# A product kernel whose moving tiles begin a few words behind an aligned place

## The chip, the cores and the metric

The kernel runs on one core of a Trainium2 chip. The metric is the device time of one execution in microseconds (us). On this core TensorE multiplies, VectorE and ScalarE do elementwise work and take results out of PSUM, and the SP queue issues the DMAs. SBUF is the memory on the chip that the engines read; a place in it is given here as a partition's byte address, and a word is 4 bytes.

## What is computed

The reference chains an attention, a gated layer and a mixture of eight experts over 2304 tokens of 512 values. Only the last part touches the change:

```python
P = balanced(softmax-like weights of x @ w_gate)      # 2304 x 8
out = 0
for e in range(8):
    h = np.maximum(x @ w1[e], 0.0)                    # 2304 x 1024
    out += P[:, e:e + 1] * (h @ w2[e])                # 2304 x 512
```

The first matrix of an expert is w1, the second is w2.

## The kernel before, in words

Every product is made in a split form: a number is written as a high part (`hi`, in TensorE's one-pass format float32r) and a low part (`lo`, what is left), and three one-pass matmuls, high by high, high by low and low by high, stand for one of full precision. `split` (L146) makes the two parts: ScalarE casts the raw values to the high part (L147), VectorE subtracts it from the raw values and gives the low part (L148).

The program has these stages by time. Up to about 365 us there are attention and the gated layer. From about 380 to 550 us the experts run over the first 256 tokens with plain products (`up0`, L1029 and L1032, and `down0`, L1061). From about 560 us to the end they run over two groups of 1024 tokens each; this is the stage that the change is in.

In that last stage an expert's half is one step `s`, 32 steps in all (16 to 47). Both products of a step are made in Strassen's manner, with seven products of half-size matrices in place of eight, numbered 1 to 7. `up` (L1188, matmuls L1202) multiplies by w1, `down7` (L1136, matmuls L1154) by w2. `moe_step` (L1418) weaves them: for each of seven numbers it runs `up` for step s, 2 times 6 matmuls, and then `down7` for step s-1, 2 times 6 matmuls. So there are 32 times 7 times 12 = 2688 matmuls in L1154 and as many in L1202, all with 128 by 128 weights and 512 moving columns.

In `down7` the weights are the parts of w2 (`w`), and what moves through TensorE are the scaled hidden values of the tokens, 512 tokens in a row: `r[:, c]`, where `r` is a tile `hi` or `lo` of shape 128 by 2 by 512. For a product, the six matmuls of one output bank read hi, lo, hi of the first half (c = 0) and hi, lo, hi of the second (c = 1).

These tiles are made in `h_forms` (L1095), a generator. Its inner function `form(p, x)` takes two tiles from pools `hi` and `lo` with three buffers each, 4096 bytes of a partition, and calls `split`. `moe_step` steps the generator once ahead of each `down7`, after one step ahead of the loop, so the tiles of a number are asked for one number ahead of their matmuls. For five of the seven numbers the generator makes differences of the raw blocks in place first (L1109, L1110, L1116, L1124).

The order on TensorE, VectorE and ScalarE is the order in which the program is written. Two small tiles, `edge` (L129) and `rim` (L130), are set once and not used; they only take room. With them, every moving and every stationary operand of the matmuls in float32r, from the gated layer to the end, begins at a multiple of 64 bytes in the built program. The three `hi` tiles begin at 175872, 179968 and 184064, the three `lo` tiles at 163584, 167680 and 171776, the tiles `xf` that move in L1202 at 69120 and each 8192 further on. The identity matrix `ident`, which moves in plain float32 in the attention stage (L211, L299), begins at 1184, 32 bytes behind such a place.

Of the kernel before, what the change touches and what calls it, by code (L numbers as in the profile page):

```python
# [10 lines left out]
F32R = mybir.dt.float32r  # L11
# [13 lines left out]
NB = 512  # L25
# [4 lines left out]
CONV = 0.6  # L30
TW = 384
LATE = 4
AHEAD = 3

WID = [512, 512, 512, 512]
# [69 lines left out]
def fused_kernel(  # L105
# [17 lines left out]
    def pool(name, bufs, **kw):  # L123
        st = ExitStack()
        return st.enter_context(tc.tile_pool(name=name, bufs=bufs, **kw)), st

    const, _ = pool("const", 1, side="left"); ctx.enter_context(_)
    edge, _ = pool("edge", 1, side="right"); ctx.enter_context(_)
    nc.gpsimd.memset(edge.tile([128, 56], F32, name="edge"), 0.0)  # L129
    nc.gpsimd.memset(const.tile([128, 8], F32, name="rim"), 0.0)  # L130
    wp, _ = pool("wp", 16, side="left"); ctx.enter_context(_)
# [14 lines left out]
    def split(hi, lo, raw, eng=dve):  # L146
        act.copy(out=hi, in_=raw)  # L147
        eng.tensor_tensor(out=lo, in0=raw, in1=hi.bitcast(F32), op=ALU.subtract)  # L148
# [634 lines left out]
    def dord(s):  # L783
        return LORD if s == NS - 1 else DORD
# [3 lines left out]
    st, closers = {}, {}  # L788
# [4 lines left out]
    def open_(name, n, side="right", tag=None, keep=False):  # L793
        st[name], closers[name] = pool(tag or name, n, side=side, reuse_waits="tile")
        if keep:
            ctx.enter_context(closers[name])
# [8 lines left out]
    def load_w2(s, j, name="r2"):  # L805
        _, e, fh = steps[s]
        t = st[name].tile([128, 2, DM], F32, tag=name, name=f"r2_{s}{j}")
        r0 = FH * fh + 256 * j
        nc.sync.dma_start(t, w2[e, r0:r0 + 256, :].rearrange("(f p) d -> p f d", p=128))
        raw2[s, j] = t  # L810
# [82 lines left out]
    def w1_get(s, p):  # L893
        if p not in (1, 2, 4):
            wf[s, p] = get(w1d, s, p)
        else:
            t = unit([128, 2, 2, 256], F32R, f"w1f{s}_{p}")
            split(t[:, 0], t[:, 1], raw1.pop((s, p)))
            wf[s, p] = t
# [82 lines left out]
    def x_tile(g, p):  # L982
        if (g, p) not in xf:
            xf[g, p] = st["xf"].tile([128, 2, 2, NB], F32R, tag="xf", name=f"xf{g}{p}")
        return xf[g, p]
# [65 lines left out]
    def down0(s, tt):  # L1051
# [12 lines left out]
        if fh == 0:  # L1064
            return
        if e < LATE:
            acc[e, tt] = st["acc"].tile([128, DM], F32, tag="acc", name=f"acc{e}{tt}")
# [3 lines left out]
        dst = acc[0, tt]  # L1071
        if e == LATE:
            dve.tensor_scalar_mul(dst, dst, pr[:, 0:1])
# [4 lines left out]
    def combine():  # L1078
        for i in range(1, LATE):
            for tt in range(2):  # L1080
                dve.scalar_tensor_tensor(acc[0, tt], acc[i, tt], prob["P"][:, T0[tt][2], i:i + 1], acc[0, tt],
                                         op0=ALU.mult, op1=ALU.add)
                yield
# [11 lines left out]
    def h_forms(s):  # L1095

        b11, b12, b21, b22 = (hb[s, f, t] for f in range(2) for t in range(2))

        def form(p, x):
            hi = st["hi"].tile([128, 2, NB], F32R, tag="hi", name=f"hi{s}_{p}")  # L1100
            lo = st["lo"].tile([128, 2, NB], F32R, tag="lo", name=f"lo{s}_{p}")
            split(hi, lo, x)
            hf[s, p] = hi, lo

        form(1, b11)
        yield
        form(3, b22)
        yield
        dve.tensor_tensor(b11, b12, b11, op=ALU.subtract)  # L1109
        dve.tensor_tensor(b12, b22, b12, op=ALU.subtract)  # L1110
        if dord(s) is DORD:
            form(7, b12)
            yield
        form(5, b11)
        yield
        dve.tensor_tensor(b22, b22, b11, op=ALU.subtract)  # L1116
        form(6, b22)
        yield
        if dord(s) is LORD:
            form(7, b12)  # L1120
            yield
        form(2, b21)
        yield
        dve.tensor_tensor(b21, b21, b22, op=ALU.subtract)  # L1124
        form(4, b21)
        yield
# [229 lines left out]
    with tc.manual_schedule(engines={mybir.EngineType.PE, mybir.EngineType.DVE, mybir.EngineType.Activation}):  # L1356
        for i, (c, b) in enumerate(seq):
# [14 lines left out]
            for half in range(2):  # L1372
# [27 lines left out]
                if ahead:  # L1400
# [4 lines left out]
                    n = tiles.pop(0)  # L1405
                    gemm2_wide(*n, None, pump, tiles[0])
                    second()
                while len(tiles) > keep:
                    n = tiles.pop(0)
# [8 lines left out]
    def moe_step(s):  # L1418
# [3 lines left out]
        for n, p in enumerate(ORD):  # L1422
            if s < NS:
                for i in range(2):
                    up(s, i, p)
                if swap:
                    nc.sync.dma_start(x_tile(2, p).bitcast(F32), xfd[p])
                q = 7 * s + n + AHEAD
                if q < 7 * NS:
# [7 lines left out]
            if s == G0 and n == 0:  # L1437
                load_w2(G0, 0, "r1")
                load_w2(G0, 1, "r1")
            q = 7 * (s - 1) + n + AHEAD  # L1440
            if G0 <= q // 7 < 2 * G0:
# [15 lines left out]
    with tc.manual_schedule(engines={mybir.EngineType.PE, mybir.EngineType.DVE, mybir.EngineType.Activation}):  # L1457
# [9 lines left out]
        for name, n in (("xf", 7), ("cp", 5), ("xr", 2), ("pb", 2)):  # L1467
            open_(name, n, side="left", keep=True)
        open_("acc", 2 * LATE)
        st["u0"], u0_st = pool("pu", 2, space=PSUM, side="left", reuse_waits="tile")  # L1470
# [7 lines left out]
        for s in range(G0 + 1):  # L1478
            for j in range(2):
                g, n, h, m = (w2s, s, w1s, s + 2) if j else (w1s, s + 1, w2s, s)  # L1480
# [10 lines left out]
                if s < G0:  # L1491
                    adv(g, n, 4)
                    adv(h, m, 1)
                    if s > 0:
                        next(sk, None)
                    if s > 2 * LATE + 2:
                        next(comb, None)
# [10 lines left out]
            if s == G0 - 1:  # L1508
                for p in ORD[:AHEAD]:
                    w1_get(G0, p)  # L1510
# [66 lines left out]
```

## Time and profile before

| | |
|---|---|
| time, median of 3 runs | 1775.88 us (1775.6 to 1777.68) |
| the profiled execution | 1775.71 us, its span 1773.9 us |
| TensorE busy | 1759.1 us, 99% of the span |
| VectorE busy | 1453.2 us, 82% |
| ScalarE busy | 1085.9 us, 61% |
| chain that ended last, by engine | TensorE 95%, VectorE 2%, DMA 1%, ScalarE 1% |
| the same by line | L1154 34%, L1202 20% + 10% + 5% |
| granted clock of TensorE | 1.00 in every stretch read |

The profiled execution's time is 1.8 us more than its span, which is what lies around it. A matmul's duration in the profile (389 ns for 512 columns) goes from its beginning to a modelled end and overlaps the next; what a matmul costs in a row of matmuls is the distance from its start to the next one's start, which is read from the length of a piece of several.

### The profile page before, as it was taken

The page shows a single profiled execution, that of the slowest core. Times are in us where ns is not written, and L with a number is a line of the kernel's source. Part 1 is how long each engine was busy: PE and PEld are TensorE (multiplying, and loading weights), DVE is VectorE, ACT ScalarE, POOL GpSimd, SP SyncE. Part 2 cuts the span into 40 slices and gives each one's busy share as a digit, 9 for nine tenths or more (in the row PEclk, how much of TensorE's full clock was granted, in tenths as well). Part 3 has the DMA queues.
Part 4 walks back from the last instruction along what each step waited for, and adds up shares of the span by engine and source line. Part 5 has one row for each costly group of instructions (what it writes and reads, how often), then busy time and mean ns, then how long its engine had stood idle before and what let it go on. Part 6 is the DMA issues. An engine that isn't in the chain of part 4 may idle for free.

```text
span 1773.9 us, 24849 instructions
## 1 busy us (share of the span) xinstructions
PE 1759.1 (99%) x9320; PEld 1492.3 (84%) x9320; DVE 1453.2 (82%) x1954; ACT 1085.9 (61%) x1737; POOL 1.1 (0%) x10
## 2 busy tenths in 40 slices
PE   7999999999999999999999999999999999999999
PEld 4999999988888888888888888888888888888887
DVE  7968797668996989998889999887777777777778
ACT  6776675655664666656666666655555555555555
POOL 0000000000000000000000000000000000000000
PEclk9999999999999999999999999999999999999999
DMA  9226776866674755456454556955455444545442
GB/s 381 113 96 226 251 272 253 328 215 189 203 245 146 266 178 177 167 206 208 161 178 167 179 194 205 318 189 173 159 170 170 150 158 143 172 155 172 148 131 95
DMA packets 141000, 341.72 MB, mean 193 GB/s; under 512 B 11840, under 2 KB 49104, under 8 KB 139984
## 3 DMA queue, kind: packets, MB, share of 16 engines
q1 hardware_dynamic: 140880, 340.14, 56.0%
q8 instruction: 73, 1.20, 0.3%
q14 instruction: 47, 0.39, 0.1%
HBM read 256.66 MB, written 83.44 MB: 192 GB/s over the span
## 4 chain that ended last, share of the span: by engine, by line
PE 95%; DVE 2%; DMA 1%; ACT 1%; issue 0%; SPq 0%; DVEq 0%
PE d L1154 34%; PE X L1202 20%; PE Z L1202 10%; PE g2w L712 8%; PE g L619 5%; PE d L1061 5%; PE Y L1202 5%; PE u L1029 3%; PE g L675 3%; PE u L1032 2%; DMA kq<-in_qT_dram 1%; PE u L197 1%; DMA rawin<-in_moe_w_in_dram 0%; PE lg L1236 0%; PE s L197 0%
## 5 line engine op out<-in xcount | busy, mean ns | idle before, releaser
L148 DVE TENSOR_TENSOR lo<-hb,hi 128x1024 fp32r<-128x1024 f32 x224 | 273.8, 1222 | 32.7 <-ACT hi L147 31.9
L1154 PE MATMUL d<-hi,w2f 128*128 128x512 f32 x896 | 294.4, 389 | 0.0
L1202 PE MATMUL X<-xf,w1l 128*128 128x512 f32 x1152 | 276.9, 389 | 0.0
L147 ACT CAST hi<-hb 128x1024 fp32r<-128x1024 f32 x224 | 235.2, 1051 | 66.4 <-PE d L1154 60.9
L1202 PEld LDWEIGHTS X<-xf,w1l 128*128 128x128 f32 x1152 | 216.3, 188 | 44.8
L1162 ACT COPY M<-d 128x512 f32<-128x512 f32 x235 | 137.8, 588 | 140.1 <-PE d L1154 139.2
L1166 DVE TENSOR_TENSOR M<-d,M 128x512 f32<-128x512 f32 x203 | 139.9, 690 | 100.0 <-PE d L1154 99.9
L1154 PEld LDWEIGHTS d<-hi,w2f 128*128 128x128 f32 x896 | 168.1, 188 | 34.8
L1154 PE MATMUL d<-lo,w2f 128*128 128x512 f32 x448 | 174.4, 389 | 0.0
L1154 PE MATMUL d<-hi,w2l 128*128 128x512 f32 x512 | 167.9, 390 | 0.0
L712 PE MATMUL g2w<-ring,woh 128*128 128x384 f32 x576 | 147.0, 336 | 0.2 <-DVE U L584 0.2
L1150 ACT COPY d<-M 128x512 f32<-128x512 f32 x217 | 127.6, 589 | 21.4 <-DVE M L1166 20.2
L1154 PE MATMUL d<-hi,w2g 128*128 128x512 f32 x384 | 125.8, 389 | 0.0
L1154 PEld LDWEIGHTS d<-hi,w2l 128*128 128x128 f32 x512 | 96.2, 188 | 20.3 <-ACT d L1150 0.4
L712 PEld LDWEIGHTS g2w<-ring,woh 128*128 128x128 f32 x576 | 102.9, 188 | 4.9 <-issue 3.4
L1209 ACT COPY cp<-X 128x512 f32<-128x512 f32 x128 | 74.4, 582 | 47.1 <-PE X L1202 47.0
L1154 PE MATMUL d<-lo,w2l 128*128 128x512 f32 x256 | 99.7, 389 | 0.0
L1154 PEld LDWEIGHTS d<-lo,w2f 128*128 128x128 f32 x448 | 84.2, 188 | 17.5
L1202 PE MATMUL Y<-xf,w1f 128*128 128x512 f32 x384 | 97.3, 389 | 0.0
L712 PE MATMUL g2w<-ring,wol 128*128 128x384 f32 x288 | 96.3, 334 | 0.0
L147 ACT CAST w1f<-rb 128x512 fp32r<-128x512 f32 x96 | 59.8, 624 | 56.9 <-PE d L1154 43.1
L1202 PE MATMUL X<-xf,w1f 128*128 128x512 f32 x384 | 92.2, 389 | 0.0
(216 smaller groups left out, 3399.3 us busy)
## 6 DMA issues: line engine op xcount, KB each, us to landing
r<-in_moe_w_dram SPq DMA_DIRECT2D x128, 512.0 KB, 4.0
w1l<-w1d SPq DMA_DIRECT2D x128, 512.0 KB, 3.9
w1d<-po SPq DMA_DIRECT2D x64, 512.0 KB, 4.4
w2d<-w2f SPq DMA_DIRECT2D x64, 512.0 KB, 4.1
w2l<-w2d SPq DMA_DIRECT2D x64, 512.0 KB, 3.4
rb<-in_moe_w_dram SPq DMA_DIRECT2D x96, 256.0 KB, 2.6
sb<-in_moe_w_dram SPq DMA_DIRECT2D x48, 256.0 KB, 2.6
pb<-pd SPq DMA_DIRECT2D x16, 512.0 KB, 5.3
```

What stands on the lines that cost most here:

```text
L147: act.copy(out=hi, in_=raw)
L148: eng.tensor_tensor(out=lo, in0=raw, in1=hi.bitcast(F32), op=ALU.subtract)
L619: pe.matmul(ps, lhs[:, fs], rhs, start=(n == 0), stop=(n == 5))
L675: pe.matmul(ps[:, :HS], lhs, rhs, start=(n == 0), stop=(n == 3 * nf - 1))
L712: pe.matmul(ps[:, :TW], lhs[:, f % 2, ds], ring[f // 2][:, 2 * (f % 2) + rhs, q], start=(n == 0 and not on), stop=(n == 11), skip_group_ch ...
L1061: pe.matmul(ps, h[:, l, f % 2, 128 * tt:128 * tt + 128], w[:, f % 2], start=(fh == 0 and n == 0), stop=(fh == 1 and n == 11))
L1150: act.copy(out=ps, in_=m)
L1154: pe.matmul(ps, w[:, l, c, 128 * d:128 * d + 128], r[:, c], start=(n == 0 and not seed), stop=(n == 5), skip_group_check=seed)
L1162: act.copy(out=m, in_=ps)
L1166: dve.tensor_tensor(m, ps, m, op=ALU.add)
L1202: pe.matmul(ps, w[:, l, c, 128 * i:128 * i + 128], x[:, r, c], start=(n == 0 and p in (1, 7)), stop=(n == 5), skip_group_check=p in (2, 6, ...
L1209: act.copy(out=t, in_=ps)
```

## The change

Each `hi` and `lo` tile becomes 16 words longer, and the 1024 words in use begin behind the tile's beginning, by the number p of the product: 1 word for product 1, 2 for 3, 4 for 7, 6 for 5, 10 for 6, 12 for 2 and 14 for 4. It holds for the write of both parts, for VectorE's reading of the high part, and for the matmuls' moving operand.

```diff
 LATE = 4
+SHIFT = {1: 1, 3: 2, 7: 4, 5: 6, 6: 10, 2: 12, 4: 14}
 AHEAD = 3
 ...
         def form(p, x):
-            hi = st["hi"].tile([128, 2, NB], F32R, tag="hi", name=f"hi{s}_{p}")
-            lo = st["lo"].tile([128, 2, NB], F32R, tag="lo", name=f"lo{s}_{p}")
+            hi, lo = (st[k].tile([128, 2 * NB + 16], F32R, tag=k, name=f"{k}{s}_{p}")[:, SHIFT[p]:SHIFT[p] + 2 * NB]
+                      .rearrange("p (t n) -> p t n", t=2) for k in ("hi", "lo"))
             split(hi, lo, x)
             hf[s, p] = hi, lo
```

In the built program the tiles themselves still begin at multiples of 64 bytes (`hi` at 175680, 179840 and 184000, `lo` at 163200, 167360 and 171520), so the moving operands of products 1, 3, 7, 5, 6, 2 and 4 begin 4, 8, 16, 24, 40, 48 and 56 bytes behind one, 384 matmuls each. The two tiles `rb` lie 384 bytes lower, still at multiples of 64 bytes. All other tiles stay where they were.

The instructions of all five engines stand in the same order as before, in the same number. One wait differs: since the slots move, the first `lo` tile that touches the room of an earlier tile `acc`, whose store is a DMA, is another one. On VectorE at the beginning of the last stage (`lo_3`, `lo_7`: the low parts of products 3 and 7; `hb`: the raw hidden values; `S`, `w2f`: sums and parts of w2; `cp`: copies of `up`), before:

```order
L148 TENSOR_TENSOR lo_3_6388<-hb_6283,hi_3_6387 128x1024 [waits Activation_49]
L829 TENSOR_TENSOR S_2_6321<-S_1_6319,r_160_6214 128x512 [waits DVE_49]
L1109 TENSOR_TENSOR hb_6224<-hb_6307,hb_6224 128x1024
L829 TENSOR_TENSOR S_4_6323<-r_161_6216,S_2_6321 128x512 [waits DVE_49]
L1110 TENSOR_TENSOR hb_6307<-hb_6283,hb_6307 128x1024 [waits DVE_49]
L148 TENSOR_TENSOR w2f_3_6325<-S_4_6323,w2f_3_6325 128x512 [waits Activation_49]
L1225 TENSOR_TENSOR cp_6243<-Z_6257,cp_6243 128x512 [waits PE_49]
L148 TENSOR_TENSOR lo_7_6435<-hb_6307,hi_7_6434 128x1024 [waits DMAHW7_49,Activation_49]
```

The same place with the change:

```order
L149 TENSOR_TENSOR lo_3_6388<-hb_6283,hi_3_6387 128x1024 [waits DMAHW7_49,Activation_49]
L830 TENSOR_TENSOR S_2_6321<-S_1_6319,r_160_6214 128x512 [waits DVE_49]
L1110 TENSOR_TENSOR hb_6224<-hb_6307,hb_6224 128x1024
L830 TENSOR_TENSOR S_4_6323<-r_161_6216,S_2_6321 128x512 [waits DVE_49]
L1111 TENSOR_TENSOR hb_6307<-hb_6283,hb_6307 128x1024 [waits DVE_49]
L149 TENSOR_TENSOR w2f_3_6325<-S_4_6323,w2f_3_6325 128x512 [waits Activation_49]
L1226 TENSOR_TENSOR cp_6243<-Z_6257,cp_6243 128x512 [waits PE_49]
L149 TENSOR_TENSOR lo_7_6435<-hb_6307,hi_7_6434 128x1024 [waits Activation_49]
```

The wait for the DMA (DMAHW7) stands at product 3's tile now, one product earlier; the line numbers are one higher since a line is added at the top.

## Rows read from the trace of the kernel before

**Rows 1.** The page: busy time by engine, and the chain by engine and line.

```profile
PE 1759.1 (99%) x9320; PEld 1492.3 (84%) x9320; DVE 1453.2 (82%) x1954; ACT 1085.9 (61%) x1737; POOL 1.1 (0%) x10
...
PE 95%; DVE 2%; DMA 1%; ACT 1%; issue 0%; SPq 0%; DVEq 0%
PE d L1154 34%; PE X L1202 20%; PE Z L1202 10%; PE g2w L712 8%; PE g L619 5%; PE d L1061 5%; PE Y L1202 5%; PE u L1029 3%; PE g L675 3%; PE u L1032 2%; DMA kq<-in_qT_dram 1%; PE u L197 1%; DMA rawin<-in_moe_w_in_dram 0%; PE lg L1236 0%; PE s L197 0%
```

**Rows 2.** Windows of the last stage: busy us of each engine, granted clock, DMA.

```profile
620.00:1180.00 560.00, 560.00 (x2472) 463.78 (x2471) 502.22 (x668) 350.26 (x553) 0.00 (x0) 1.00 0.57 195
1240.00:1740.00 500.00, 500.00 (x2208) 414.30 (x2207) 380.59 (x473) 281.10 (x433) 0.00 (x0) 1.00 0.49 157
```

**Rows 3.** Line L1154: duration min/median/max in ns; then what it waited for.

```profile
L1154 PEld LDWEIGHTS d<-hi,w2f x896: 187/188/188, 572.3 to 1178.5; 128*128 128x128 f32 x180
L1154 PE MATMUL d<-hi,w2f x896: 388/389/398, 572.5 to 1178.7; 128*128 128x512 f32 x180
...
its engine sat idle before it (us, times) until:
  ACT d L1150: 0.4, 1
```

**Rows 4.** The chain in order of time, last stage: start us, us, what.

```profile
561.59 5.44 PE X L1202 x24
...
572.69 2.72 PE d L1154 x12
...
610.77 2.76 PE d L1154 x12
```

**Rows 5.** The chain in the gated layer: 288 columns (L619), 384 columns (L712).

```profile
158.84 3.19 PE g L619 x24
...
169.38 8.33 PE g2w L712 x48
```

**Rows 6.** The chain in the plain expert stage, 512 columns (L1061).

```profile
384.19 2.75 PE d L1061 x12
...
418.56 2.78 PE d L1061 x12
```

**Rows 7.** Timeline of TensorE: plain float32, 128 columns of ident; duration in ns.

```profile
10.18 1.83 PE L211 MATMUL warm<-ident 128*128 128x128 f32 x14
...
L211 PE MATMUL warm<-ident x50: 275/275/378, 10.2 to 34.5; 128*128 128x128 f32 x50
```

**Rows 8.** The page: the casts and subtractions of L147 and L148.

```profile
L148 DVE TENSOR_TENSOR lo<-hb,hi 128x1024 fp32r<-128x1024 f32 x224 | 273.8, 1222 | 32.7 <-ACT hi L147 31.9
...
L147 ACT CAST hi<-hb 128x1024 fp32r<-128x1024 f32 x224 | 235.2, 1051 | 66.4 <-PE d L1154 60.9
```

**Rows 9.** L490, L484, L485: 1024 elements in steps of two words, ns min/median/max.

```profile
L490 DVE SCALAR_TENSOR_TENSOR win<-rawin,win x6: 1214/1218/1226, 95.2 to 226.5; 128x1024 uint32<-128x1024 uint32 x6
...
L484 ACT ACTIVATE win<-rawin x6: 1124/1140/1147, 92.6 to 220.4; 128x1024 f32<-128x1024 f32 x6
...
L485 ACT ACTIVATE rawin<-rawin x6: 1112/1144/1176, 93.7 to 221.4; 128x1024 uint32<-128x1024 uint32 x6
```

**Rows 10.** The store of acc, its landing, and the low part of product 3.

```profile
L1076 SPq DMA_DIRECT2D out_dram<-acc x2: 337/338/338, 548.8 to 551.5; - x2
...
DMA to landing us min/median/max: 2.1/2.3/2.5
...
569.90 1.23 DVE L148 TENSOR_TENSOR lo<-hb,hi 128x1024 fp32r<-128x1024 f32 x1
```

## The prediction

> **What bounds the kernel now.** I read the page first: TensorE is busy 99% of the span, and the chain that ended last runs 95% on it, 34% in L1154 alone, which is the only line whose operands the change moves [rows 1]. Next the windows of the last stage. In 560 and in 500 us of it TensorE is busy to the last microsecond at a granted clock of 1.00, VectorE 502 of 560 and ScalarE 350 of 560 in the denser stretch [rows 2]. Then what L1154 waited for: in the whole program 0.4 us, once, for the seed of a bank, and never for a `hi` or a `lo` [rows 3]. So TensorE sets the time, every nanosecond that a matmul of L1154 gains or loses is gained or lost at the end, and nothing that is lost there can be caught up.
>
> What one matmul costs I take from distances between starts, in the chain in order of time: 24 matmuls of 512 columns in 5.44 us are 226.7 ns each, 12 of L1154 in 2.72 us the same [rows 4]. In the gated layer 288 columns cost 3.19/24 = 132.9 ns and 384 columns 8.33/48 = 173.5 ns [rows 5]. [...]
>
> **The change part by part.**
>
> *Order, counts, memory.* No instruction is added, removed or moved, so there is no term for order. The 384 bytes more hold nothing else. The tile `rb` stays at a multiple of 64 bytes, and I price its loads as before: 0.
>
> *The moved wait.* VectorE's first `lo` of product 3 now waits for the store of `acc`. The later of the two stores is issued at 551.5 us and lands 2.1 to 2.5 us later, by 554.4; that `lo` begins at 569.9 [rows 10]. The wait is over 15 us before: 0. Had it held, the sums and differences queued behind it on VectorE would have come later, and TensorE's first matmuls of product 3 with them.
>
> *ScalarE writes and VectorE reads and writes at an odd word or off a multiple of 16 bytes.* The trace shows no write of this kind. The nearest rows are reads in steps of two words: VectorE reads the odd words in 1218 ns for 1024 elements, no more than the 1222 ns of L148 for aligned runs [rows 8, 9]; ScalarE reads the odd words in 1140 ns and the even ones in 1144 [rows 9]. I take 0. For the bound: if each of the 224 subtractions took a quarter more, 1222/4 = 306 ns, the stretch from 620 to 1180 us, with 2472/168 = 14.7 steps (168 matmuls in a step) and so 103 of them, would have 31 us more work on VectorE, and VectorE has 560 - 502 = 58 us free there. The cover is also one of order: the parts of a number are made one number ahead, 24 matmuls or 5.4 us, and ScalarE's casts wait for TensorE (60.9 of 66.4 us [rows 8]), which is to say that they wait for a buffer, not TensorE for them. [...]
>
> *The moving operand of 2688 matmuls.* This is the term. In before every float32r operand begins at a multiple of 64 bytes, so no row shows the price of another beginning. [...] Zero: the extra reading is absorbed. Above: 512 words from an unaligned start touch one more piece of memory than from an aligned one, whatever the size of the pieces in which they are read, and a piece of k words is worth k column times. Pieces of 4 words: five of the seven offsets (1, 2, 6, 10, 14) are off, 1920 x 4 x 0.417 = 3.2 us. Pieces of 8 words: all seven offsets are off, 2688 x 8 x 0.417 = 9.0 us. Pieces of 16 words: 2688 x 16 x 0.417 = 17.9 us.
>
> [...] Second, in the plain expert stage, where the same 512 columns are not met in a steady row, they cost 2.75/12 = 229.2 to 2.78/12 = 231.7 ns, 2.5 to 5.0 more than the steady 226.7 [rows 6]. Third, a group of L1154 that was once out of step took 2.76 instead of 2.72 us, 3.3 ns a matmul, and the time was not made up behind it [rows 4]. So a matmul that is put out of step loses some 3 to 5 ns, and the piece of 8 words, 3.3 ns, lies within that. I take 3.33 ns for each of the 2688: 9.0 us. The ends that I keep are 0 and 17.9 us.
>
> Sum, against the profiled execution: 1775.71 + 9.0 = 1784.7 us. The median of the runs shown is 1775.88, 0.01% away, so nothing is to be added for that. About 0.2%, 3.6 us, is what a measurement of this kernel can tell from no change.
>
> **The rivals.**
>
> *No price (not slower).* The reading runs ahead of the columns far enough that a piece more vanishes while the weights change. [...] It decides when the operand's reader is idle while the weights go in. Time 1775.7.
>
> *Pieces of four words.* The price is there, but only 3.2 us: 1778.9, within 0.2%. [...] No row here shows it.
>
> [...]
>
> [...]
>
> *The parts come too late.* A write off its place makes casts and subtractions longer than VectorE's free time and TensorE waits. It decides from 58/103 = 0.56 us per subtraction on, nearly half of 1222 ns more; I price it at 10 us and over, 1786.
>
> **How the numbers follow.** A price of 8 to 16 words, or of falling out of step, for all products: 0.42, the forecast. No price: 0.35. Pieces of four words: 0.09. The odd word: 0.07. Faster: 0.05. Parts too late: 0.02. Slower by over 0.2% is 0.42 + 0.07 + 0.02 = 0.51; within 0.2% is 0.35 + 0.09 = 0.44; faster 0.05. The range goes from no price less a spread of the runs, 1774.5, to pieces of 16 words, 1793.6, and a little of falling out of step beside them, 1797. It leaves out the odd word, the faster case, the late parts and the outermost of the forecast, some 0.16. For the forecast alone it would be 1780 to 1797. Signs being so near each other, the step that I trust least is the choice between absorbed and not absorbed.
>
> **What would show it.** Distances between starts in L1154, product by product, beside those of L1202, which should stay at 226.7. The forecast wants about 230.0 in all seven products (12 in 2.76 us); pieces of four words 228.3 in five and 226.7 in products 7 and 2; the odd word some 440 in product 1 alone; no price 226.7 everywhere. If TensorE shows idle time before L1154 with VectorE's L148 as the releaser, the parts are late. The prediction is wrong as a whole if the time moves while the distances in L1154 stay, or if L1202 lengthens as much as L1154: then it is not the moving operand's beginning.

## The result, and the profile with the change

With the change the kernel takes 1800.26 us (median of 4 runs, 1799.98 to 1800.55), beside 1776.15 us for the kernel before (4 runs, 1775.6 to 1777.68): a ratio of 1.0134 with an interval of 1.0117 to 1.0152. It is 24 us slower. The forecast was 9 us slower, 1784.7, with a range to 1797.0; the direction was right, the size was not, and the forecast's cause is only a part of the real one.

The page of the changed kernel (its lines are one higher than before's). First busy time by engine and the chain by engine and line, then groups: line, engine, operation, count, busy us and mean ns of one, and the idle time before them with its releaser.

```profile
PE 1784.2 (99%) x9320; PEld 1495.5 (83%) x9320; DVE 1456.3 (81%) x1954; ACT 1085.7 (60%) x1737; POOL 1.1 (0%) x10
...
PE 97%; DMA 1%; DVE 1%; ACT 0%; SPq 0%; issue 0%; DVEq 0%
PE d L1155 35%; PE X L1203 20%; PE Z L1203 10%; PE g2w L713 8%; PE g L620 6%; PE d L1062 5%; PE Y L1203 5%; PE u L1030 3%; PE g L676 3%; PE u L1033 2%; PE u L198 1%; DMA kq<-in_qT_dram 1%; DMA rawin<-in_moe_w_in_dram 0%; PE lg L1237 0%; PE s L198 0%; DVE nmx L278 0%
...
L149 DVE TENSOR_TENSOR lo<-hb,hi 128x1024 fp32r<-128x1024 f32 x224 | 273.7, 1222 | 35.4 <-ACT hi L148 35.2
L1155 PE MATMUL d<-hi,w2f 128*128 128x512 f32 x896 | 300.4, 396 | 0.0
L1203 PE MATMUL X<-xf,w1l 128*128 128x512 f32 x1152 | 279.5, 391 | 0.0
L148 ACT CAST hi<-hb 128x1024 fp32r<-128x1024 f32 x224 | 235.0, 1050 | 70.2 <-PE d L1155 65.6
```

TensorE is busy 25.1 us longer in as many instructions, 1784.2 for the 1759.1 of [rows 1], and VectorE, ScalarE and the count of everything are as they were. The casts and subtractions that now write and read off their old place last 1050 and 1222 ns, as in [rows 8]. TensorE sat idle in front of L1155 once, as in [rows 3]:

```profile
its engine sat idle before it (us, times) until:
  ACT d L1151: 0.3, 1
```

So nothing waits for anything that it did not wait for before; the matmuls themselves follow each other more slowly, and the profile gives each of L1155 396 ns in place of 389 [rows 3]. The windows of the last stage (busy us and count for PE, PEld, DVE, ACT, POOL, then granted clock, DMA share, GB/s) show it most simply:

```profile
620.00:1180.00 560.00, 560.00 (x2423) 455.71 (x2422) 492.20 (x653) 348.97 (x550) 0.00 (x0) 1.00 0.54 190
1240.00:1740.00 500.00, 500.00 (x2164) 406.94 (x2163) 375.43 (x465) 275.68 (x425) 0.00 (x0) 1.00 0.46 154
```

In the second window 2164 matmuls go through where 2208 did [rows 2], at the same granted clock of 1.00. That is 500/2164 = 231.1 ns each instead of 226.4, 4.6 ns more, and over the 5376 matmuls of both lines 24.8 us: the whole loss. The chain in order of time (start us, us, what) tells which line has it:

```profile
1450.02 2.81 PE d L1155 x12
1452.84 2.73 PE X L1203 x12
1455.56 2.80 PE d L1155 x12
1458.37 2.75 PE Z L1203 x12
1461.11 2.81 PE d L1155 x12
1463.92 2.75 PE X L1203 x12
```

Both have it. A group of twelve of L1155 takes 2.80 to 2.81 us, 233 to 234 ns a matmul, and the group of L1203 behind it 2.73 to 2.75, 227.5 to 229, though none of L1203's operands was moved. Added up over all distances from one matmul's start to the next, measured against 226.67 ns, L1155 pays 18.7 us (mean 233.65 ns) and L1203 6.0 us (mean 228.9). By product the means in L1155 are 236.3 ns for product 1 (4 bytes), 235.2 for 3 (8), 231.9 for 7 (16), 231.9 for 5 (24), 235.4 for 6 (40), 231.9 for 2 (48) and 233.1 for 4 (56).

Below, "extra" is always such a sum of distances above 226.67 ns, in L1154/L1155 (here called down) and in L1202/L1203 (up); up to four distances of over 300 ns in a run, where TensorE waits, are left out. Where a beginning modulo 256 bytes is given, it is the one in the built program. Edits are against the changed kernel, unless it is said that they are against the one before.

### The profile page after: what moved, and what is told of

It is laid out like the page before. It is cut to its first block, busy times and chain, and to the rows that moved or that the text cites. A ratio compares the mean times of both kernels' runs of the same rounds, so it can differ in the third digit from the quotient of the medians.

```text
span 1798.5 us, 24849 instructions
## 1 busy us (share of the span) xinstructions
PE 1784.2 (99%) x9320; PEld 1495.5 (83%) x9320; DVE 1456.3 (81%) x1954; ACT 1085.7 (60%) x1737; POOL 1.1 (0%) x10
## 4 chain that ended last, share of the span: by engine, by line
PE 97%; DMA 1%; DVE 1%; ACT 0%; SPq 0%; issue 0%; DVEq 0%
PE d L1155 35%; PE X L1203 20%; PE Z L1203 10%; PE g2w L713 8%; PE g L620 6%; PE d L1062 5%; PE Y L1203 5%; PE u L1030 3%; PE g L676 3%; PE u L1033 2%; PE u L198 1%; DMA kq<-in_qT_dram 1%; DMA rawin<-in_moe_w_in_dram 0%; PE lg L1237 0%; PE s L198 0%; DVE nmx L278 0%
## 5 line engine op out<-in xcount | busy, mean ns | idle before, releaser
L149 DVE TENSOR_TENSOR lo<-hb,hi 128x1024 fp32r<-128x1024 f32 x224 | 273.7, 1222 | 35.4 <-ACT hi L148 35.2
L1155 PE MATMUL d<-hi,w2f 128*128 128x512 f32 x896 | 300.4, 396 | 0.0
L1203 PE MATMUL X<-xf,w1l 128*128 128x512 f32 x1152 | 279.5, 391 | 0.0
L148 ACT CAST hi<-hb 128x1024 fp32r<-128x1024 f32 x224 | 235.0, 1050 | 70.2 <-PE d L1155 65.6
L1203 PEld LDWEIGHTS X<-xf,w1l 128*128 128x128 f32 x1152 | 216.4, 188 | 48.3
L1155 PEld LDWEIGHTS d<-hi,w2f 128*128 128x128 f32 x896 | 168.9, 188 | 39.9
L1155 PE MATMUL d<-lo,w2f 128*128 128x512 f32 x448 | 177.1, 395 | 0.0
L1155 PE MATMUL d<-hi,w2l 128*128 128x512 f32 x512 | 171.1, 396 | 0.0
L1155 PE MATMUL d<-hi,w2g 128*128 128x512 f32 x384 | 128.4, 396 | 0.0
L1155 PEld LDWEIGHTS d<-hi,w2l 128*128 128x128 f32 x512 | 96.5, 189 | 23.1 <-ACT d L1151 0.3
L1155 PE MATMUL d<-lo,w2l 128*128 128x512 f32 x256 | 101.3, 396 | 0.0
L1155 PEld LDWEIGHTS d<-lo,w2f 128*128 128x128 f32 x448 | 84.7, 189 | 19.3
L1203 PE MATMUL Y<-xf,w1f 128*128 128x512 f32 x384 | 98.4, 392 | 0.0
L148 ACT CAST w1f<-rb 128x512 fp32r<-128x512 f32 x96 | 59.6, 622 | 60.8 <-PE d L1155 46.6
L1203 PE MATMUL Z<-xf,w1f 128*128 128x512 f32 x384 | 93.1, 391 | 0.0
```

Source lines behind the costliest of these rows:

```text
L1155: pe.matmul(ps, w[:, l, c, 128 * d:128 * d + 128], r[:, c], start=(n == 0 and not seed), stop=(n == 5), skip_group_check=seed)
L1203: pe.matmul(ps, w[:, l, c, 128 * i:128 * i + 128], x[:, r, c], start=(n == 0 and p in (1, 7)), stop=(n == 5), skip_group_check=p in (2, 6, ...
```

## Experiments

### One shift for all products

```diff
-SHIFT = {1: 1, 3: 2, 7: 4, 5: 6, 6: 10, 2: 12, 4: 14}
+SHIFT = dict.fromkeys(range(1, 8), 8)    # and likewise 4, 2, 1
```

> All seven products begin 8 words (32 bytes) behind a multiple of 64 bytes. Theory A, the place within 32 bytes sets the price: no price, 1776 us (1774 to 1779), L1155 and L1203 both at 226.7 ns from start to start. Rival B, every beginning off a multiple of 64 bytes pays one piece more: about as the changed kernel, 1795 to 1805 us. Rival C, the change of place from product to product is what costs, not the place: no price here and none in any kernel with one place for all.

> All products begin 4 words (16 bytes) behind a multiple of 64. Theory A, with the price that product 7 had at this place in the changed kernel (63 ns in its 12 matmuls and 27 ns in the 12 of the next up): 224 x 90 ns = 20 us, 1796 us. Theory of pieces of four words (16 bytes): 1776. Rival C (change of place): 1776. Rival D, one piece of eight words more for every place off 32 bytes, alike for all places: the changed kernel's 24 us, 1800.

> All products begin one word (4 bytes) behind. Theory A with product 1's price (115 ns in its group, 36 in the next): 224 x 151 ns = 34 us, 1810 us. Rival D (alike for all places): 1800. Rival C: 1776.

> All products begin two words (8 bytes) behind. Theory A with product 3's price (103 ns in its group, 36 in the next; product 6, 40 bytes behind, had 104 and 11): 224 x 115 to 139 ns = 26 to 31 us, 1802 to 1807 us. Rival D: 1800. Rival C: 1776.

| shift | time us | ratio, interval | down mean ns, extra us | up extra us |
|---|---|---|---|---|
| 8 words (32 bytes) | 1797.04 | 1.0118, 1.0103 to 1.0133 | 232.6, 16.0 | 5.7 |
| 4 words | 1795.08 | 1.0109, 1.0092 to 1.0125 | 231.9, 14.0 | 5.8 |
| 2 words | 1806.16 | 1.0169, 1.0154 to 1.0185 | 235.2, 23.0 | 7.9 |
| 1 word | 1808.8 | 1.0185, 1.0169 to 1.02 | 236.2, 25.6 | 8.0 |

All four are in the change's slots of 4160 bytes, whose own price comes next. Every shift costs more than the 9.0 us of the forecast, 1 and 2 words the most, and up always pays too. There is no step between "on a piece" and "off a piece": 4 words and 8 words cost nearly the same. The chain with one word:

```profile
1453.22 2.73 PE X L1203 x12
1455.95 2.82 PE d L1155 x12
1458.78 2.77 PE X L1203 x12
```

### The longer tiles without a shift

The change does two things: the columns move, and the slots become 4160 bytes instead of 4096. The first kernel keeps only the longer slots. The second has slots of 4352 bytes, 17 times 256, and no shift; the third has these slots and the change's seven shifts.

```diff
 s0_pad
-SHIFT = {1: 1, 3: 2, 7: 4, 5: 6, 6: 10, 2: 12, 4: 14}
+SHIFT = dict.fromkeys(range(1, 8), 0)
 P0_wide_pad: the same, and
-            hi, lo = (st[k].tile([128, 2 * NB + 16], ...
+            hi, lo = (st[k].tile([128, 2 * NB + 64], ...
 Porig_wide_shift: the second edit alone
```

> The tiles are 16 words longer and lie where they lie in the changed kernel, but all products begin at the tile's beginning, a multiple of 64 bytes. Theory E, the price is paid for every moving operand off a multiple of 64 bytes and depends on how far off: 1776 us (1774 to 1779), all distances 226.7 ns. Rival F, the price is that of the longer tiles (other addresses, no longer multiples of 128): 1795 to 1800.

> The tiles are 64 words longer than before, so that each slot is 17 x 256 bytes and begins at a multiple of 256 as before; no shift. Theory J, what counts is the beginning of the moving operand within 256 bytes: 1776 us (1774 to 1779), every distance 226.7 ns. Rival F2, longer tiles or other addresses cost whatever their multiple: 1795 to 1800.

> The changed kernel's seven shifts (1, 2, 4, 6, 10, 12, 14 words) on slots that begin at multiples of 256. Theory J: a price for each product off 256, about the changed kernel's 24 us, 1796 to 1804. Rival K, the changed kernel's loss came from its slots alone (they begin 64, 128 or 192 bytes behind a multiple of 256) and shifts of less than 64 bytes add nothing of their own: 1776.

Without any shift the slots of 4160 bytes give 1799.54 us (1.0133, 1.0118 to 1.0148): extra 15.3 us in down and 8.7 in up. My theory of that moment, that only a beginning off a multiple of 64 bytes costs, fell with this run, since all its tiles begin at such multiples. With slots of 4352 bytes and no shift it is 1775.94 (0.9999, 0.999 to 1.0008). The chains, first the slots of 4160, then those of 4352:

```profile
1455.15 2.79 PE d L1155 x12
1457.94 2.75 PE Z L1203 x12
1460.69 2.80 PE d L1155 x12
```

```profile
692.19 2.72 PE d L1155 x12
694.91 2.72 PE X L1203 x12
697.63 2.72 PE d L1155 x12
```

So the length of a tile costs nothing by itself (4352 bytes); that with slots of 4160 bytes five of the six begin 64, 128 or 192 bytes off a multiple of 256 does. In the kernel before, `hi` and `lo` all begin at multiples of 256 bytes: 175872 is 687 x 256, 163584 is 639 x 256, and the slots are 4096 long. So do the tiles `xf`: 69120 is 270 x 256. The prediction went by multiples of 64 alone.

With these good slots the seven shifts alone cost as much again: 1798.84 (1.0124, 1.0109 to 1.0139), extra 18.3 in down and 5.2 in up. Either half of the change brings nearly the whole loss, and both together 24.1 us: the prices don't add.

### Is it the reader or the writers?

Here `xf`, which moves in up and is made ahead of a token group's steps, is moved by 16 bytes, once with `hi` and `lo` as in the kernel with longer slots and no shift, once with all of `hi` and `lo` moved by 16 bytes too. The slots of `xf` become 64 bytes longer with that.

```diff
 x4_up_only
+SHIFT = dict.fromkeys(range(1, 8), 0)
+XSHIFT = 4
-            xf[g, p] = st["xf"].tile([128, 2, 2, NB], F32R, tag="xf", ...
+            t = st["xf"].tile([128, 4 * NB + 16], F32R, tag="xf", ...
+            xf[g, p] = t[:, XSHIFT:XSHIFT + 4 * NB].rearrange(...)
 xh4_both: the same with SHIFT 4 for all
```

> hi and lo begin on 64 bytes as before, the tiles xf that move in up begin 16 bytes behind. These are written once in a token group, so ScalarE and VectorE write nothing off its place within a step. Theory E (TensorE's reading): as with all products of down7 16 bytes behind, roles exchanged: 13 to 15 us in up's own matmuls, 5 to 6 in those of down7, 1794 to 1797 us. Rival G, the writes of the casts and subtractions off their place are what disturbs TensorE: 1776.

> hi, lo and xf all begin 16 bytes behind, so each of the 5376 matmuls of the last stage does. Theory E with a price of each matmul's own reading: 5376 x 5.2 ns = 28 us and nothing after it, 1802 to 1806 us, at a mean distance of 231.9 ns. Rival H, what costs is the passing from operands on one place to operands on another: the distance settles at 226.7 after each stall, 1776 us.

They gave 1803.21 (1.0155, 1.0138 to 1.0172) and 1805.73 (1.0168, 1.0153 to 1.0183); the first is more than expected, since the slots alone cost too. The chain with `xf` alone moved, in which up takes what down takes:

```profile
1454.82 2.79 PE X L1205 x12
1457.61 2.76 PE d L1157 x12
```

Beside the kernel with longer slots and no shift, up's extra rises from 8.7 to 14.6 us where `xf` is moved, and down's falls from 15.3 to 13.2. Beside the shift of 4 words, up's rises from 5.8 to 15.6 and down's stays (14.0, 14.8). So up pays when its own moving operand is moved, as down does, though no engine writes `xf` beside these matmuls. With the unchanged casts and subtractions above, this speaks against the writers and for TensorE's reading. W32 below, in which no write is moved at all and the loss is as large (1800.36 us), shows it.

### One matmul of twelve

Against the kernel before, only the second half of product 7's `lo` is moved by 16 bytes; all `lo` slots are 4160 bytes long for it.

```diff
-            lo = st["lo"].tile([128, 2, NB], F32R, tag="lo", name=f"lo{s}_{p}")
+            gap = 4 if p == 7 else 0
+            lo = (st["lo"].tile([128, 2 * NB + 16], ...)[:, :2 * (NB + gap)]
+                  .rearrange("p (t n) -> p t n", t=2)[:, :, :NB])
```

> Only the second half of product 7's lo begins 16 bytes behind, one matmul in each six of that product, 64 in the whole program. Theory E2, the price has two parts, a stall at the one matmul and a row of matmuls after it that are out of step although their operands lie well: the one and the next 8 to 10 cost 25 to 35 ns together beyond 226.7 each, 64 x 30 = 1.9 us in all. Rival: only the one matmul is longer, by 3 to 10 ns, 0.2 to 0.6 us in all.

It gave 1789.52 (a single time). The slots spoilt what it was meant to show, since most of the cost is in products that it did not move, but the slots themselves tell something. Where a `lo` tile begins 128 bytes off a multiple of 256, the distances run 226, 235, 226, 226, 235, 226: each of the two `lo` matmuls costs some 8 ns more, and the row stays in step. Where it begins 64 or 192 bytes off, the whole group falls out of step.

### Is it the place, or the place beside the others?

Against the kernel before: `edge` is a tile that only takes room on the right side of SBUF, `rim` one on the left. Making `edge` 128 bytes longer moves `hi` and `lo` by 128 bytes, and leaves `xf` and the weights. Making both longer by 128, or both by amounts that move everything by 32 modulo 256, moves all operands and keeps their places to each other.

```diff
 E32_right_128
-    nc.gpsimd.memset(edge.tile([128, 56], F32, name="edge"), 0.0)
+    nc.gpsimd.memset(edge.tile([128, 88], F32, name="edge"), 0.0)
 RE32_all_128: the same, and
-    nc.gpsimd.memset(const.tile([128, 8], F32, name="rim"), 0.0)
+    nc.gpsimd.memset(const.tile([128, 40], F32, name="rim"), 0.0)
 RE8_all_32: edge 112 words, rim 16 words
```

> The unused tile edge is 32 words longer, so every tile on the right side of SBUF lies 128 bytes lower: hi and lo begin 128 bytes behind a multiple of 256, xf and the weights at multiples of 256 as before (the stage at 380 to 550 us has its moving xs and its stationary h0 moved too). Theory J: L1154 costs some 8 ns more a matmul, as the lo tiles did that lay so in the kernel with one matmul moved, 2688 x 8 = 21 us, 1795 to 1800, and L1202 stays at 226.7. Rival F3, the price needs a beginning off 128 bytes: 1776.

> Both unused tiles are 32 words longer, so moving and stationary operands of all matmuls lie 128 bytes further off a multiple of 256, and keep their places to each other. Theory J1, the place of the moving operand itself: L1202 and L1154 pay both, 2 x 21 us, 1815 to 1820. Theory J2, the place of the moving operand against that of the weights that are loaded beside it: 1776 (1774 to 1779), all at 226.7 ns.

> Unused tiles so sized that moving and stationary operands of all matmuls lie 32 bytes behind where they lay, off 64, 128 and 256 alike, and keep their places to each other. Theory J2: 1776 us (1774 to 1779). If a beginning off 64 bytes has a price of its own (the prediction's step): 1785 us or more.

`hi` and `lo` alone 128 bytes on: 1796.47 (1.0111, 1.0094 to 1.0128), extra 16.0 in down and 3.3 in up; the distances in down alternate between 229 and 237 to the end of each group. Everything 128 bytes on: 1776.6 (1.0001, 0.9992 to 1.001). Everything 32 bytes on: 1777.08 (1.0001, 0.9991 to 1.0011). The chain with only `hi` and `lo` moved, then windows with all moved by 128, and by 32 bytes:

```profile
1452.82 2.79 PE d L1154 x12
1455.61 2.73 PE Z L1202 x12
1458.35 2.79 PE d L1154 x12
```

```profile
1240.00:1740.00 500.00, 500.00 (x2208) 414.01 (x2207) 380.68 (x473) 281.20 (x433) 0.00 (x0) 1.00 0.47 157
```

```profile
1240.00:1740.00 500.00, 500.00 (x2207) 414.17 (x2206) 380.57 (x474) 281.09 (x434) 0.00 (x0) 1.00 0.49 157
```

With everything moved as many matmuls go through as before [rows 2]. So a beginning at 128 or at 32 modulo 256 has no price of its own. What costs with `hi` and `lo` alone moved is that one operand of the row stands 128 bytes off the other. That up would stay at 226.7 ns there, as was expected, did not hold: its first three matmuls behind each group of down pay.

The same kernel moved `xs` and `h0` of the plain stage, each beside an operand that stayed. L1061 takes 232.8 ns a matmul there for 230.1 before, L1029 233.3 for 230.9; L1032, whose rows have 256 columns, 118.4 for 118.4 (from the starts of the single matmuls). So the narrower row pays nothing.

### Moving the weights

The weight tiles of down are read at `128 * d` words. In W0, W32, Wsame and W4 they are read at `64 * d` and some words on, which keeps the number and size of the weight loads and lets the beginning be chosen. These four therefore multiply by other weight columns than the reference. W0 moves nothing (against the kernel before), W32 moves the weights alone by 128 bytes (against the kernel before), Wsame lets the weights follow the change's seven shifts. P4 moves `hi` and `lo` by 16 bytes in slots of 4352 bytes, with the weights as they are, and W4 moves the weights by 16 bytes with them.

```diff
 Wsame_weights_follow: 2 * NB + 64 as in Porig_wide_shift, and
-                    pe.matmul(ps, w[:, l, c, 128 * d:128 * d + 128], r[:, c],
+                    pe.matmul(ps, w[:, l, c, 64 * d + SHIFT[p]:64 * d + SHIFT[p] + 128], r[:, c],
 W32_weights_only: 64 * d + 32        W0_slices_only: 64 * d
 P4_moving_16: 2 * NB + 64, SHIFT 4 for all
 W4_both_16: as Wsame_weights_follow, SHIFT 4 for all
```

> The two kernels with moved weight columns took the columns of the four weight tiles of L1154 in steps of 64 words instead of 128, so that they overlap. This kernel takes them in such steps with no move at all; the weights used are in part others, so its numbers are not those of the reference. Theory: only places count, so 1776 and 226.7 ns everywhere. Rival: the overlapping columns themselves had a price, so 1790 or more, and what was concluded from the two kernels falls.

> hi, lo and xf as before at multiples of 256 bytes; only the weight columns of down7 are taken 32 columns (128 bytes) further on, or back (outputs not the reference's). Theory J2: the same price as with hi and lo moved by 128 bytes and the weights left, 1796 us, with L1154 alternating near 229 and 238 ns. Theory J1: 1776 us.

> As the wide pad with the seven shifts, but the 128 weight columns that a matmul of down7 loads begin as many words behind a multiple of 256 bytes as its moving operand does (other columns of the same tile, so the outputs are not the reference's; the count and size of the matmuls stay). Theory J2, moving operand against weights: down7 falls back to 226.7 ns, and what is left stands where down7 and up meet, 448 places with one or two matmuls of some 8 ns and a few after them: 1776 to 1784 us. Theory J1, the moving operand's own place: as without it, 1798.8 us. By where the rest stands: if the own weights count, nothing is left at the meeting places; if the weights that are loaded beside a running matmul (those of the next) count, the last matmul of each piece pays.

> Moving tiles of L1154 begin 16 bytes on for all seven products, in slots that are multiples of 256 bytes. Theory (a moving operand that stands elsewhere than its weights costs 2 to 10 ns, and the aligned matmuls behind a group pay some): 1795 to 1800, L1154 near 232, L1202 near 228.5. Rival (the changes between products were the price, here there are none): under 1785.

> As the kernel with moving tiles 16 bytes on, and the weight columns of L1154 begin 16 bytes on too (steps of 64 words, other weight columns, so its numbers are not those of the reference). Rival a, only moving against its own weights counts: 1776 to 1782, L1154 226.7. Theory b, the change of place from one group of twelve to the next is what costs: 1790 to 1800 with L1154 falling back towards 226.7 inside each group. Theory c, what counts is the place against all other operands: L1154 stays at 230 to 233 to the end of each group.

| what is moved | time us | ratio, interval | down mean ns, extra us | up extra us |
|---|---|---|---|---|
| nothing, columns overlap (W0) | 1776.11 | 0.9999, 0.999 to 1.0009 | 226.7, 0.2 | 0.0 |
| weights alone, 128 bytes (W32) | 1800.36 | 1.0135, 1.012 to 1.015 | 233.0, 16.9 | 8.1 |
| both, by product (Wsame) | 1799.92 | 1.0132, 1.0117 to 1.0148 | 232.8, 16.3 | 8.0 |
| moving alone, 16 bytes (P4) | 1795.41 | 1.0105, 1.0088 to 1.0122 | 231.5, 12.9 | 6.3 |
| both, 16 bytes (W4) | 1790.32 | 1.0078, 1.0063 to 1.0093 | 230.2, 9.6 | 5.2 |

Overlapping columns cost nothing. The weights alone, 128 bytes off the rest, cost as much as the moving operand 128 bytes off the rest and more, and L1154 does not alternate between 229 and 238 ns as was expected. The distance from the last up matmul to the first of such a group, in which the first of the moved weights are loaded (in L1154 a weight load begins 0.2 us ahead of its matmul, 572.3 and 572.5 us in [rows 3]), is already 5.8 ns longer. The chain with W32, and with P4:

```profile
1455.62 2.80 PE d L1154 x12
1458.42 2.76 PE Z L1202 x12
1461.17 2.80 PE d L1154 x12
```

```profile
1452.83 2.78 PE d L1155 x12
1455.60 2.75 PE Z L1203 x12
1458.35 2.78 PE d L1155 x12
```

W32 beside RE32 does not fit a reading of the weights that has nothing to do with that of the moving operand: weights at 128 bytes cost nothing where the moving operands stand there too (1776.6 us), and 24 us where they don't (1800.36). What the two share, no run tells.

Letting the weights follow the moving columns does not restore the pace, against the 1776 to 1784 us that were expected of it. With the seven shifts it helps in some products and not in others; extra ns a matmul, moving alone (Porig) and both (Wsame): 4 bytes 10.8 and 10.6, 8 bytes 8.1 and 5.0, 16 bytes 4.8 and 3.6, 24 bytes 6.9 and 6.9, 40 bytes 5.5 and 6.0, 48 bytes 6.7 and 4.6, 56 bytes 4.8 and 5.9. With one shift of 16 bytes it is clearest. The chain with W4:

```profile
1453.69 2.76 PE d L1155 x12
1456.45 2.74 PE X L1203 x12
...
1464.70 2.76 PE d L1155 x12
1467.47 2.74 PE X L1203 x12
1470.21 2.76 PE d L1155 x12
```

Position by position (mean over the groups of twelve, ns above 226.67), worked out from the starts of the single matmuls:

| | down, matmuls 1 to 12 | up behind it, 1 to 12 |
|---|---|---|
| moving alone (P4) | 5.9 3.3 0.9 7.5 8.3 3.3 0.9 7.5 8.3 3.3 0.8 7.4 | 4.2 4.2 9.2 1.6 5.8 4.1 0 0 0 0 0 0 |
| both (W4) | 5.7 1.7 5.0 1.7 5.0 1.7 5.0 1.7 5.0 1.7 5.0 3.4 | 3.4 9.1 1.7 5.8 4.2 0 0 0 0 0 0 0 |

Two things are to be seen. In up, where all operands stand where they stood before, the row is back at 226.7 after five or six matmuls; it pays only for having been put out of step. In down it does not come back: with both moved it alternates between 5.0 and 1.7 to the end, a mean of 3.35 ns. That is eight times the 0.419 ns that one column more costs between 288 and 512 columns: (226.7 - 132.9)/224 [rows 4, 5]. A change of place from group to group alone, after which a row comes back as up does, doesn't explain that.

Nor do the matmuls of up that lie between. Behind up's last group the program has 96 matmuls of down in a row, and their first 36 run without a wait. In W4 every operand of that row, moving or weight, begins at 16 modulo 256. The timeline (start us, us) before, in W4 and in W32, each from one `lo` matmul to the one 24 matmuls on:

```profile
1747.67 0.39 PE L1154 MATMUL d<-lo,w2g 128*128 128x512 f32 x1
...
1753.11 0.39 PE L1154 MATMUL d<-lo,w2l 128*128 128x512 f32 x1
```

```profile
1762.13 0.39 PE L1155 MATMUL d<-lo,w2g 128*128 128x512 f32 x1
...
1767.65 0.39 PE L1155 MATMUL d<-lo,w2l 128*128 128x512 f32 x1
```

```profile
1772.24 0.40 PE L1154 MATMUL d<-lo,w2g 128*128 128x512 f32 x1
...
1777.81 0.39 PE L1154 MATMUL d<-lo,w2l 128*128 128x512 f32 x1
```

That is 5.44, 5.52 and 5.57 us for 24 matmuls. Over 33 distances of this row the mean is 226.7 ns before, in P0 and W0, and with everything moved by 32 or by 128 bytes; 230.0 with both at 16 bytes (W4); 231.5 with the moving operand alone at 16 bytes (P4); 232.1 with the weights alone at 128 (W32) and 233.5 with the moving operand alone at 128 (E32). So there are two prices in a row, and up is needed for neither: one for a moving operand and weights at different places modulo 256, and one of 3.3 ns for a beginning at 16 bytes, where 32 and 128 are free, even if both share it.

## Why the prediction was wrong, step by step

**What bounds the kernel: right.** TensorE hardly ever waits (busy 99% of the span), and what a matmul loses is lost at the end: 24.7 us of extra distances are 24.6 us of span (1798.5 less 1773.9).

**Order, moved wait, writers: right.** All three were priced at 0. The idle time in front of L1155 is a single 0.3 us, as before 0.4, the casts and subtractions last as long as before, and the rival of late parts has nothing for it. The odd word costs VectorE nothing either: over all products 1222 ns is the mean and 1229 the most, and with all seven products one word on (s1_all) the mean is 1223.

**"The 384 bytes more hold nothing else", and the beginnings as multiples of 64: the step that failed first.** I took it that the tiles, still at multiples of 64 bytes, were as good as before, and gave the longer slots no price at all. They alone cost 23 us (s0_pad), and 0 at a multiple of 256 (P0_wide_pad). The forecast's own sentence "In before every float32r operand begins at a multiple of 64 bytes, so no row shows the price of another beginning" stopped too early: in the last stage they all begin at the same place modulo 256, and that is what the change broke twice, by its slots and by its shifts. One row of before did have operands at two places: L619 reads its 288 columns from 0 and from 128 modulo 256, beside weights at 0. They cost 132.9 ns each in a full row [rows 5]; by place, 132.6 ns is the mean of those that read from 0 and 132.8 of those from 128 (distances within L619, those over 200 ns left out). So this price is shown for 512 columns, and not for so few.

**The moving operand of 2688 matmuls: mis-sized, and only a part of the cause.** The term was one more piece of 8 words at 0.417 ns a column, 3.33 ns, 9.0 us; L1155 pays 7.0 ns, 18.7 us. No run shows that a moving operand is read in pieces, nor the 0.417 ns; one column more costs 0.419 ns in [rows 4, 5], and what the runs show in the term's place is a cost by where moving operand and weights begin. A price of that size does exist: 3.3 ns where moving operand and weights share a beginning at 16 bytes (W4), and none at 32 (RE8), as pieces of 8 words would have it. That is in part luck, since the size was chosen for lying among the 3 to 5 ns of falling out of step; and whether the moving operand or the weights bring it, no run tells. What the term left out is the place of the moving operand against the weights. Moving the weights and leaving the moving operand costs 25 us of distances (W32), so no reckoning by pieces of the moving operand alone can be right. Nor do pieces of 8 words give the 10.6 ns of a beginning at 4 bytes with the weights following (Wsame).

**What [rows 7] can't show.** The 14 records of its first line are not at one pace: one distance of 214 ns and twelve of 111 or 112. Both their operands are `ident`, so they share one place, and the row could not show the price of two. That a beginning 8 words off costs nothing where all operands share it is shown by RE8 (1777.08 us, 1.0001), and this row, in plain float32, does not carry it for float32r. How the 226.7 ns of a matmul in float32r divide into its columns and the rest, no run shows.

**"L1202, which should stay at 226.7": wrong.** It pays 6.0 us. The forecast had the row that says so: a group that fell out of step took 2.76 us in the kernel before [rows 4], and the rows of the plain stage cost 2.5 to 5 ns more [rows 6]. I used them to support a size, 3 to 5 ns, and did not ask what falling out of step is: a state of the whole row of matmuls, carried over to the next group whatever that reads (P4: the first six matmuls of up pay 4.2, 4.2, 9.2, 1.6, 5.8 and 4.1 ns). In the plain stage of before, where all operands begin at multiples of 256 bytes, L1061 falls out of step behind the rows of 256 columns in L1032: 235, 233, 236, 224, 231, 236, 228, 233, 231, 226 and 227 ns (from 418.40 us on). The same sequence is seen in the last stage at full pace: with P0, after one disturbance at 623 us, the distances are 230, 238, 233, 236, 224, 231, 236, 228, 233, 231 and then 226 or 227 again. In the last stage of before such a disturbance is rare (0.1 us of extra in all); the change makes one in each of 224 groups. By the forecast's own sign it was wrong as a whole if L1202 lengthened as much as L1154; it lengthened by a third of that, 2.2 for 7.0 ns, so a price of the moving operand was in it.

**The rivals.** No price fell: the change costs 24 us; whether the operand's reading runs ahead of the columns, no run tells. Pieces of four words fell: 16 bytes, which that rival holds to be free, cost 18.9 us on good slots (P4), and beside the other shifts those of 16 and 48 bytes cost 4.8 and 6.7 ns a matmul (Porig). The odd word fell: product 1 runs at 236 ns, not 440, though it is the dearest of the seven. Faster fell: no run shows a row of 512 columns that stays under 226 ns a matmul.

**The range.** Its upper end was made of pieces of 16 words and "a little of falling out of step". With falling out of step taken as a state of both lines, at its own 3 to 5 ns for 5376 matmuls, it would have reached 16 to 27 us, 1792 to 1803, and held the time.

**What stays open.** Why a row of 512 columns is slower with moving operand and weights 128 bytes apart modulo 256 (E32 1796.47 us, W32 1800.36) than with both at one place (RE32 1776.6, P0 1775.94, W0 1776.11) is not shown by any run. Why a beginning at 16 bytes costs 3.3 ns even where it is shared is open as well, and so is why 4 and 8 bytes cost the most (10.8 and 8.1 ns on good slots, beside 4.8 to 6.9 for the other five). How the two prices and the row's falling out of step add up to the change's 24 us was not worked out: slots and shifts each cost 23 us alone. None of the kernels was faster than before.

## What to carry to other kernels

Where TensorE is the bound and its rows of 512 columns run without a gap, look at the beginnings of all operands, the moving ones and the weights, modulo 256 bytes. Keep them at one common place, and choose one that was free here: 0, 32 or 128 (P0 1775.94, RE8 1777.08, RE32 1776.6 us); at 16 a row ran at 230.0 ns a matmul, not at 226.7 (W4). Keep slots multiples of 256 bytes (4352 bytes cost nothing, 4160 cost 23 us), and don't mix tiles with small shifts into a row (Porig, 1798.84 us on good slots). A tile that grew by 16 words cost as much here as the shift of the data in it, and the loss showed not as idle time but in the matmuls' own durations (396 for 389 ns) and distances (233.65 for 226.7 ns). When a profile shows a row that is "out of step" once, ask what would make it so always, and price that over every line of the row, not over the line that is changed.

## What the runs showed of the hardware that was not expected

A common shift of all operands by 32 or by 128 bytes costs nothing (both 1.0001), and one operand class 128 bytes off the rest costs 1.1 to 1.4% of the whole kernel (`hi` and `lo` 1.0111, weights 1.0135). A row whose operands all begin at 16 bytes runs at 230.0 ns, not at 226.7 (W4's last matmuls). The distance ahead of the first moved weights is already 5.8 ns longer (W32). A row that was out of step came back by itself in five to ten matmuls where its operands shared a free place (up behind W4's and P4's groups five or six, P0 at 623 us ten); with moving operand and weights 128 bytes apart it did not within the 36 that run without a wait (232.1 ns in W32, 233.5 in E32). Rows of 256 and of 288 columns paid nothing for operands 128 bytes apart (L1032 118.4 ns in E32 as before; L619 132.6 from 0 and 132.8 from 128).
